# Sliding-window attention with a gated two-layer MLP on one core: w_in in three parts ahead of batch 1's Q and K, V's tail read once, the last PV inside stage one of tile 1

## The chip, the cores and the metric

One NeuronCore of a Trainium2 chip. The metric is the device time of one execution in microseconds (us). A profile's span is some 1.8 us shorter than the time of the same execution. Engines: PE is the matmul array (PEld its weight loads), DVE VectorE, ACT ScalarE, POOL GpSimd, SP SyncE.

## The reference

```python
# q, k, v: (8, 8, 576, 64) float32; w_in (512, 2048), w_out (2048, 512)
scores = q @ k.transpose(0, 1, 3, 2) / 8
rel = pos[:, None] - pos[None, :]
scores = where((rel >= 0) & (rel < 64), scores, -1e9)
a = softmax(scores) @ v
x = a.transpose(0, 2, 1, 3).reshape(4608, 512)
h = x @ w_in
out = (h * clip(h + 3, 0, 6) / 6) @ w_out
```

## The kernel before

The tokens are worked through in nine tiles of 512. For each, stage one (`s1`) makes 16 chunks of gated hidden features, four 512-column matmuls each, and stage two (`s2`) 16 chunks of output of the same size. The attention of later batches is fitted between these chunks, so that PE has work while DVE and ACT evacuate. A sequence of 576 is 4 blocks of 128 and a tail of 64 ("rest rows"; the attention work on those of batch 0 is called small). Scores are Q times K, PV is the softmax weights times V, a bank (h, o, acc or st) is one of PE's result buffers, and an evacuation is the copy out of one. A number in a line name such as L633 is a line of the kernel that ran, so the same code has other numbers in the other kernels.

The loads of weights and of batch 1 are all issued by POOL, into one queue, in this order:

```python
w_in = [load_w_in(0, 512, 0, NG)]
bt.cast_v(...); bt.cast_v(...)
w_in.append(load_w_in(512, 1024, 0, NG))
bt.cast_v(...)
w_in.append(load_w_in(1024, 1536, 0, NG))
ld = LoadsForPE(1, nc.gpsimd)
ld.main(0, 0, 4)                      # Q of batch 1, heads 0 to 3
ld.main(1, 0, 4)                      # K
w_in.append(load_w_in(1536, 2048, 0, NG))
ld.rest()                             # rest rows of Q and K
w_out = [load_w_out(0, 4)]
# ... later: Q and K of heads 4 to 7, w_out parts 2 and 3, rest rows of
# batch 0, w_out part 4, V of batch 1 (its last block with 128 rows)
```

The stretch that the change works on, in PE's order:

```python
run(m, 12)                            # the first chunks of stage one, tile 0
TT(bt, 0, oa_tr)                      # transposes of Q and K, head pair 0
run(m, 2)
TT(bt, 1)
run(m, 1)
RR(bt, st_tr(0))                      # transposes of the rest rows
run(m)
for h in range(0, H, 2):              # POOL: cast of V, all five blocks
    pcopy(out=bt.V[:, :, h : h + 2, 0:D], in_=vst1[:, :, h : h + 2, :])
# ...
m = s2(0, BY_PART)                    # go(n): n chunks of stage two, tile 0
go(); SS1_(0)                         # SS1_: scores, exp, mask of a pair
go(2); SS1_(1)
go(); TT(bt, 2, st_tr(0))
go(); TT(bt, 3, st_tr(1))
go(2); SS1_(2)
go(3)
SS1_(3)
go()
RR(bt0, st_tr(0))                     # batch 0's rest rows
acopy(...)                            # their V
go(2)
rest_s(bt0, 1)                        # small scores, exp, mask of batch 0's rest rows
go(2)
rest_n(bt0, 0)                        # their PV
pv_pair(bt, 0, 1)                     # PV of a head pair; X_: its transposes
go()
pv_pair(bt, 1, 0)
X_(bt, 0)
pv_pair(bt, 2, 1)
rest_x(bt0, h_tr())
X_(bt, 1, iter((tr_of(ps_o, "o"),)))
pv_pair(bt, 3, 0)
# then tile 1: m = s1(1, ...); run(m, 1); X_(.., 2); run(m, 1); X_(.., 3); ...
```

The softmax here doesn't subtract the row's maximum and nothing guards it: scores larger than these inputs give would overflow.

Of the kernel before, what the change touches and what calls it, by code (L numbers as in the profile page):

```python
# [24 lines left out]
def kernel(  # L25
# [10 lines left out]
    P = nc.NUM_PARTITIONS  # L36
    B, H, S, D = q.shape
    DM, FF = moe_w_in.shape
    NT = B * S
    NG = H // 2  # L40
    assert D == 64 and NG * P == DM and WINDOW == D
    KB = (S + P - 1) // P
    SP = KB * P
    R = 4
    SM = P * R
    SR = S - SM
# [17 lines left out]
    ps_o = ctx.enter_context(tc.tile_pool(name="ps_o", bufs=1, space=PSUM))  # L64
    ps_h = ctx.enter_context(tc.tile_pool(name="ps_h", bufs=1, space=PSUM))
    ps_acc = ctx.enter_context(tc.tile_pool(name="ps_acc", bufs=1, space=PSUM))
# [12 lines left out]
    def load_v(b, vst, h0, h1, eng=None):  # L79
        out = []  # L80
        for h in range(h0, h1):
            out.append((eng or nc.sync).dma_start(  # L82
                out=vst[:, 0 : KB - 1, h, :],
                in_=v[b, h, 0:SM, :].rearrange("(k p) d -> p k d", p=P),
            ))
        return out
# [35 lines left out]
    def load_v_by_head(b):  # L122
        vst = stage.tile([P, KB, H, D], F32, name="vst", tag="vst")
        ins = [nc.gpsimd.dma_start(
            out=vst[:, KB - 1, :, :], in_=v[b, :, S - P : S, :].rearrange("h s d -> s h d"),
        )]
        ins += load_v(b, vst, 0, H, nc.gpsimd)
        return vst, ins
# [43 lines left out]
    def keep_busy(n):  # L172
# [11 lines left out]
        out=mask1[:], in_=mask1[:], pattern=[[1, QW]], compare_op=ISGE,  # L184
# [3 lines left out]
        out=mask1[:], in_=mask1[:], pattern=[[-1, QW]], compare_op=ISGE,  # L188
# [7 lines left out]
    for o0, m0, m1 in ((0, 0, QW), (QW, 0, QW), (2 * QW, 0, QW), (3 * QW, 0, P), (3 * QW + P, WINDOW, P)):  # L196
        nc.vector.tensor_scalar(
            out=maskneg[:, o0 : o0 + m1 - m0], in0=mask1[:, m0:m1],
# [32 lines left out]
    def load_w_in(f0, f1, g0, g1):  # L231
        return nc.gpsimd.dma_start(
            out=win16[:, g0:g1, f0:f1],
            in_=moe_w_in[g0 * P : g1 * P, f0:f1].rearrange("(g p) f -> p g f", p=P),
        )

    def load_w_out(c0, c1):
        return nc.gpsimd.dma_start(
            out=wout16[:, c0:c1, :],
            in_=moe_w_out[c0 * P : c1 * P, :].rearrange("(c p) j -> p c j", p=P),  # L240
        )


    vcopy, pcopy, acopy = nc.vector.tensor_copy, nc.gpsimd.tensor_copy, nc.scalar.copy
# [95 lines left out]
    def tr_of(pool, name):  # L340
        return pool.tile([P, 1024], BF16, name=name)
# [81 lines left out]
    def pv_pair(bt, g, u):  # L423
        t = ps_st.tile([P, 2, 512], F32, name=f"st{u}")
        for h in range(2):
            pv(bt, g, h, t[:, h, :])
        ov = t[:, :, 0 : KB * VW].rearrange("p h (k w) -> p h k w", w=VW)
        rec = small.tile([P, 2, KB], F32, name="rec2")
        nc.vector.reciprocal(out=rec[:].unsqueeze(3), in_=ov[:, :, :, D:VW])
        opgs[bt.b, g] = opool.tile([P, KB, 2, D], BF16, name="opg")  # L430
        nc.vector.tensor_tensor(
            out=opgs[bt.b, g][:].rearrange("p k h d -> p h k d"), in0=ov[:, :, :, 0:D],
            in1=rec[:].unsqueeze(3).to_broadcast([P, 2, KB, D]), op=MULT,
        )
# [31 lines left out]
    def rest_n(bt, u):  # L466
        st = ps_st.tile([P, 2, 512], F32, name=f"st{u}")
        for h in range(2):
            o = st[:, h, :]
            for g in range(NG):  # L470
                nc.tensor.matmul(
                    o[0:SR, g * VW : (g + 1) * VW], lhsT=pTr[:, h, g * SR : (g + 1) * SR],
                    rhs=bt.V[:, KB - 1, 2 * g + h, :], start=True, stop=True,
                )
        ov = st[0:SR, :, 0 : NG * VW].rearrange("p h (g w) -> p h g w", w=VW)
        rec = small.tile([P, 2, KB], F32, name="rec2")
        rec = rec[0:SR, :, 0:NG]
        nc.vector.reciprocal(out=rec.unsqueeze(3), in_=ov[:, :, :, D:VW])
        nc.vector.tensor_tensor(
            out=opr[0:SR].rearrange("p g h d -> p h g d"), in0=ov[:, :, :, 0:D],  # L480
            in1=rec.unsqueeze(3).to_broadcast([SR, 2, NG, D]), op=MULT,
        )
# [27 lines left out]
    def h_bank():  # L510
        return ps_h.tile([P, 512], F32, name=h_name())

    def h_tr():
        return ps_h.tile([P, 1024], BF16, name=h_name())

    def s1_bank(fc, T):
        if T == 0:
            if fc in (6, 7, 14, 15):
                return (ps_o, ps_acc)[fc % 2].tile([P, 512], F32, name=("o", "acc")[fc % 2])[:]
            if fc in (8, 9, 12, 13):  # L520
                return ps_st.tile([P, 2, 512], F32, name=f"st{fc % 2}")[:, 0, :]
            return h_bank()[:]
        if T == 1:
            return turn()
        if T == 2:
            if fc in (8, 9):
                return ps_st.tile([P, 2, 512], F32, name=f"st{fc % 2}")[:, 0, :]
            if fc in (6, 7, 12, 13):
                return (ps_o, ps_acc)[fc % 2].tile([P, 512], F32, name=("o", "acc")[fc % 2])[:]
            return h_bank()[:]  # L530
        if T > 1 and fc < 2:
            return ps_st.tile([P, 2, 512], F32, name=f"st{fc}")[:, 0, :]
        if fc % 4 > 1:
            return h_bank()[:]
        return (ps_o, ps_acc)[fc % 4].tile([P, 512], F32, name=("o", "acc")[fc % 4])[:]
# [114 lines left out]
    def run(gen, n=10 ** 6):  # L650
        for _ in range(n):
            if next(gen, "end") == "end":
                break
# [29 lines left out]
    def X_(bt, g, banks=None):  # L683
        xt_pe(bt, g, next(banks) if banks else h_tr())()

    def TT(bt, g, banks=None):
        T_(bt, g, banks)
        do(bt, "q", g)
        do(bt, "k", g)

    def RR(bt, banks=None):
        R_(bt, banks)
        do(bt, "r")
# [13 lines left out]
    bt, st = Batch(0), stage0  # L707
# [3 lines left out]
    w_in = [load_w_in(0, 512, 0, NG)]  # L711
    bt.cast_v(vst0, 2, 4, pcopy)
    bt.cast_v(vst0, 4, 6, pcopy)
    w_in.append(load_w_in(512, 1024, 0, NG))
    bt.cast_v(vst0, 6, 8, pcopy)
    w_in.append(load_w_in(1024, 1536, 0, NG))
    ld = LoadsForPE(1, nc.gpsimd)
    ld.main(0, 0, 4)
    ld.main(1, 0, 4)
    w_in.append(load_w_in(1536, 2048, 0, NG))  # L720
    ld.rest()
    w_out = [load_w_out(0, 4)]
    pcopy(out=bt.V[0:SR, KB - 1, :, 0:D], in_=bt.V[SR:P, KB - 2, :, 0:D])

    def S0_(g, u):
# [2 lines left out]
    def T0_(g):  # L728
# [40 lines left out]
    m = s1(0, ((0, 1), (2,)))  # L769
# [11 lines left out]
        out=mask[:], in_=mask1[:].unsqueeze(1).to_broadcast([P, 2 * (KB - 1), QW])  # L781
    )
    for h in range(2):
        nc.vector.tensor_copy(
            out=mask[:, (KB - 1) * (h + 1) - 1, P:QW], in_=mask1[:, WINDOW : 2 * WINDOW],
        )
    bt, st = Batch(1), st1
    bt.cast_qk(st, 0, 0, 4, pcopy)
    bt.cast_qk(st, 1, 0, 4, pcopy)
    bt.cast_rest(st, pcopy)  # L790
    w_out += [load_w_out(4 * i, 4 * i + 4) for i in (1, 2)]
    rst0, rvst0 = load_rest_of_first()
    cast_pairs(bt, st, 4, 4)
    w_out.append(load_w_out(12, 16))
    vst1, insv = load_v_by_head(1)
    run(m, 12)

    def st_tr(u):
        t = ps_st.tile([P, 2, 1024], BF16, name=f"st{u}")
        return iter((t[:, 0, :], t[:, 1, :]))  # L800

    TT(bt, 0, oa_tr)
    run(m, 2)
    TT(bt, 1)
    run(m, 1)
    RR(bt, st_tr(0))
    run(m)

    for h in range(0, H, 2):
        pcopy(out=bt.V[:, :, h : h + 2, 0:D], in_=vst1[:, :, h : h + 2, :])  # L810
    st2, ins2 = load_for_dma(2, (0,))
    after(ins2[0], insv[3], "the values go first")
    ld = LoadsForPE(2, nc.sync)
# [9 lines left out]
    m = s2(0, BY_PART)  # L823
    def go(n=1):
        run(m, n)

    def SS1_(g):
        S1_(g, 0, 0)
        S1_(g, 1, 1)

    go()
    SS1_(0)
    go(2)
    SS1_(1)
    go()
    TT(bt, 2, st_tr(0))
# [1 line left out]
    TT(bt, 3, st_tr(1))  # L838
    go(2)
    SS1_(2)  # L840
    go(3)
    bt0.cast_rest((None, None, rst0), vcopy)
    SS1_(3)
    go()
# [1 line left out]
    acopy(out=bt0.V[SR:P, KB - 1, :, 0:D], in_=rvst0[SR:P, :, :])  # L846
    go(2)
    rest_s(bt0, 1)
    go(2)
    rest_n(bt0, 0)  # L850
    pv_pair(bt, 0, 1)
    go()
    pv_pair(bt, 1, 0)
    X_(bt, 0)
    pv_pair(bt, 2, 1)
    rest_x(bt0, h_tr())
    X_(bt, 1, iter((tr_of(ps_o, "o"),)))
    pv_pair(bt, 3, 0)

    def stage_(T, bt, pieces1, pieces2):  # L860
        if T < 3:
            m = s1(T, ((0,), (1,), (2,)))
            run(m, 1)
            X_(Batch(T), 2, oa_tr if T == 2 else st_tr(1))
            run(m, 1)
            X_(Batch(T), 3, oa_tr if T == 2 else st_tr(0))
            run(m, 1)
        else:
            m = s1(T)
        for i in range(NFC):  # L870
            run(m, 1)
            for f in pieces1.get(i, ()):
                f()
        m = s2(T, BY_BLOCK)
        for i in range(16):
            run(m, 1)
            for f in pieces2.get(i, ()):
                f()
# [42 lines left out]
    for T in range(1, NTB):  # L921
        p1, p2 = pieces(nxt)
        b = T + 2
        nxt = None
        if b < B:
# [13 lines left out]
            else:  # L939
                sts, _ = load_for_dma(b, (0, 1))  # L940
                vst = stage.tile([P, KB, H, D], F32, name="vst", tag="vst")
# [40 lines left out]
```

## Time and profile before

| | kernel before |
|---|---|
| time, median of the 3 runs given at first | 309.39 us (309.33 to 314.37) |
| span of the profile | 308.7 us |
| PE busy | 298.9 us, 97% |
| DVE, ACT, POOL busy | 57%, 57%, 32% |

In a timeline a row has its start, its length, engine, line, operation, what is written from what, and the number merged; a bracket gives the engine's idle time ahead of it and what ended it. Matmul ends are modelled about 0.17 us past the point where the next could start, so a stop counted start to start, as I do in the text, is that much longer than its bracket.

### The profile page before, as it was taken

Reading aid. Unit: us, or ns where it says so; the run is one execution under the profiler, and the core shown is the slowest. Engines: PE = TensorE matmul, PEld = TensorE weight load, DVE = VectorE, ACT = ScalarE, POOL = GpSimd, SP = SyncE. Lnnn points to the kernel's source line nnn. Section 1 sums busy time; section 2 is a strip of 40 time slices with the busy share of each in tenths; the row PEclk is TensorE's granted clock in tenths of the full one; section 3 lists DMA queues with packets and bytes.
Section 4 is the critical chain, followed back from the end, with each engine's and each line's share of the span. In section 5 each row is a group of like instructions: output and inputs, shape, how many; then the busy total and the mean of one; then the engine's idle time right before and its main releaser. Section 6 shows DMA issues by size and latency. Waiting matters only on the chain.

```text
span 308.7 us, 5635 instructions
## 1 busy us (share of the span) xinstructions
PE 298.9 (97%) x2158; PEld 150.5 (49%) x2194; DVE 174.7 (57%) x331; ACT 176.1 (57%) x266; POOL 98.5 (32%) x137
## 2 busy tenths in 40 slices
PE   8998999999999999999999999999999999999995
PEld 3454455644554454445444554455445544444444
DVE  4559644585736782677267834774477537306700
ACT  2858655686738851794179516961588157317711
POOL 4893785463534152407041704071400000000000
PEclk9999999999999999999999999999999999999999
DMA  7999999999999999999999979999910730010011
GB/s 239 192 191 258 254 203 206 244 186 288 199 220 235 220 201 200 230 218 210 196 256 210 217 162 250 220 205 156 242 51 0 132 92 0 34 70 34 0 70 68
DMA packets 140379, 52.94 MB, mean 171 GB/s; under 512 B 127584, under 2 KB 135136, under 8 KB 140352
## 3 DMA queue, kind: packets, MB, share of 16 engines
q1 hardware_dynamic: 134112, 42.94, 69.5%
q0 software_dynamic: 5824, 9.31, 14.5%
q8 instruction: 17, 0.28, 0.4%
q10 hardware_dynamic: 416, 0.33, 0.3%
q14 instruction: 10, 0.08, 0.1%
HBM read 36.83 MB, written 9.44 MB: 150 GB/s over the span
## 4 chain that ended last, share of the span: by engine, by line
PE 84%; DMA 9%; POOL 2%; SPq 1%; issue 1%; DVE 1%; ACT 0%; POOLq 0%
PE o L633 19%; PE h L567 17%; PE acc L633 17%; PE acc L567 6%; PE o L567 6%; PE st L567 6%; DMA rst<-in_k_dram 4%; PE st L364 4%; DMA wout<-in_moe_w_out_dram 3%; PE h L394 2%; DMA qst<-in_q_dram 2%; PE h L633 2%; PE h L399 1%; DMA vst<-in_v_dram 1%; SPq L82 1%
## 5 line engine op out<-in xcount | busy, mean ns | idle before, releaser
L567 PEld LDWEIGHTS <-win 128*128 128x128 bf16 x576 | 54.9, 98 | 64.5 <-DMA win<-in_moe_w_in_dram 1.2
L633 PEld LDWEIGHTS <-gT 128*128 128x128 bf16 x560 | 51.3, 98 | 57.4 <-DMA wout<-in_moe_w_out_dram 1.0
L633 PE MATMUL o<-wout,gT 128*128 128x512 bf16 x261 | 64.3, 380 | 0.7 <-issue 0.3
L567 PE MATMUL h<-xT,win 128*128 128x512 bf16 x254 | 62.4, 379 | 0.3
L633 PE MATMUL acc<-wout,gT 128*128 128x512 bf16 x245 | 58.3, 379 | 0.9 <-issue 0.5
L372 ACT ACTIVATE pT<-st 128x768 bf16<-128x768 f32 x64 | 48.5, 808 | 17.7 <-PE st L364 17.6
L575 DVE SCALAR_TENSOR_TENSOR gT<-t,st 128x512 bf16<-128x512 bf16 (+1 forms) x26 | 19.5, 767 | 56.6 <-ACT t L574 56.5
L575 DVE SCALAR_TENSOR_TENSOR gT<-t,h 128x512 bf16<-128x512 bf16 x65 | 43.8, 685 | 10.9 <-ACT t L574 10.7
L574 ACT ACTIVATE t<-h,half 128x512 bf16<-128x512 f32 x65 | 43.9, 691 | 7.7 <-PE h L567 7.5
L382 DVE TENSOR_TENSOR pT<-pT,mask 128x1536 bf16<-128x1536 bf16 x28 | 28.6, 1021 | 23.8 <-ACT pT L372 23.7
L639 ACT COPY osb<-acc 128x512 f32<-128x512 f32 x16 | 9.4, 586 | 42.7 <-PE acc L633 42.7
L253 POOL CAST V<-vst 128x2048 bf16<-128x2048 f32 (+1 forms) x10 | 13.9, 1387 | 52.5 <-DMA vst<-in_v_dram 43.4
L567 PE MATMUL st<-xT,win 128*128 128x512 bf16 x116 | 28.2, 379 | 0.9 <-DMA win<-in_moe_w_in_dram 0.8
L263 POOL CAST qn<-qst 128x512 bf16<-128x512 f32 x24 | 16.1, 709 | 40.2 <-DMA qst<-in_q_dram 38.4
L639 ACT COPY osb<-o 128x512 f32<-128x512 f32 x17 | 10.0, 589 | 29.4 <-PE o L633 28.3
L567 PE MATMUL acc<-xT,win 128*128 128x512 bf16 x98 | 25.7, 379 | 0.1
L567 PE MATMUL o<-xT,win 128*128 128x512 bf16 x95 | 25.1, 379 | 0.1
L416 DVE TENSOR_TENSOR opg<-h,rec 128x320 bf16<-128x320 f32 x48 | 23.6, 491 | 1.7
L574 ACT ACTIVATE t<-st,half 128x512 bf16<-128x512 f32 (+1 forms) x26 | 19.3, 754 | 6.0 <-PE st L567 5.6
L394 PEld LDWEIGHTS <-pT 128*128 128x128 bf16 x256 | 17.4, 97 | 7.5 <-PE h L440 0.5
L574 ACT ACTIVATE t<-acc,half 128x512 bf16<-128x512 f32 x25 | 17.2, 687 | 4.3 <-PE acc L567 3.6
L575 DVE SCALAR_TENSOR_TENSOR gT<-t,acc 128x512 bf16<-128x512 bf16 x25 | 17.1, 685 | 2.8 <-ACT t L574 2.8
(123 smaller groups left out, 301.8 us busy)
## 6 DMA issues: line engine op xcount, KB each, us to landing
out_dram<-osb SPq DMA_DIRECT2D x31, 256.0 KB, 2.5
qst<-in_q_dram SPq DMA_DIRECT2D x28, 256.0 KB, 4.8
vst<-in_v_dram SPq DMA_DIRECT2D x24, 256.0 KB, 5.3
kst<-in_k_dram SPq DMA_DIRECT2D x23, 256.0 KB, 5.5
win<-in_moe_w_in_dram POOLq DMA_DIRECT2D x4, 512.0 KB, 8.1
wout<-in_moe_w_out_dram POOLq DMA_DIRECT2D x4, 512.0 KB, 9.6
vst<-in_v_dram SPq DMA_DIRECT2D x14, 128.0 KB, 3.1
qst<-in_q_dram POOLq DMA_DIRECT2D x2, 512.0 KB, 11.9
```

The lines of the kernel that those rows point to most:

```text
L253: copy(out=self.V[:, 0 : KB - 1, h0:h1, 0:D], in_=vst[:, 0 : KB - 1, h0:h1, :])
L263: pcopy(out=n[:, g, 0 : KB - 1, :, :].rearrange("p k h d -> p k (h d)"), in_=s[:, 0 : KB - 1, 2 * g : 2 * g + 2, :].rearrange("p k h d -> ...
L364: nc.tensor.matmul(st[:, h, o0 : o0 + n], lhsT=bt.KT[h * D : (h + 1) * D, g, k0 : k0 + P], rhs=bt.QT[h * D : (h + 1) * D, g, q0 : q0 + n], ...
L372: nc.scalar.activation(out=pT[:, :, 2 * u : 2 * u + 2, 0:QW], in_=st[:, :, 0:w].rearrange("p h (k w) -> p h k w", k=2), func=EXP, scale=scale,
L382: nc.vector.tensor_tensor(out=pT[:, :, :, 0:QW], in0=pT[:, :, :, 0:QW], in1=mask[:].rearrange("p (h k) w -> p h k w", h=2), op=MULT,)
L394: nc.tensor.matmul(ob, lhsT=pT[:, h, qb, 0:P], rhs=V[:, qb, 2 * g + h, :], start=True, stop=(qb == 0),)
L416: nc.vector.tensor_tensor(out=opgs[bt.b, g][:, 0:nb, h, :], in0=ov[:, :, 0:D], in1=rec[:, 0:nb].unsqueeze(2).to_broadcast([P, nb, D]), op= ...
L567: nc.tensor.matmul(hT, lhsT=win16[:, g, fc * P : (fc + 1) * P], rhs=xT[:, g, t0 : t0 + TB], start=(g == 0), stop=(g == NG - 1),)
L574: nc.scalar.activation(out=t1[:], in_=hT, func=RELU, bias=half[:], scale=1.0 / 6.0)
L575: nc.vector.scalar_tensor_tensor(out=out, in0=t1[:], scalar=1.0, in1=hT, op0=MIN, op1=MULT,)
L633: nc.tensor.matmul(accs[ts], lhsT=gT[:, fc, ts * P : (ts + 1) * P], rhs=wout16[:, fc, :], start=(fc == 0), stop=(fc == NFC - 1),)
L639: acopy(out=osb[:], in_=accs[ts])
```

## The change

The intent: w_in comes ahead of Q and K, so that stage one need not wait for its fourth part; the first w_out part comes ahead of the rest rows; 64 rows of V that lie in two blocks are loaded once and copied on chip by ACT; the last PV fills time inside stage one. Cut to its core:

```diff
-            out=vst[:, KB - 1, :, :], in_=v[b, :, S - P : S, :]...
+            out=vst[SR:P, KB - 1, :, :], in_=v[b, :, SM:S, :]...
@@ banks of stage one's chunks in tile 0 changed to fit
-    w_in.append(load_w_in(512, 1024, 0, NG))
+    w_in.append(load_w_in(512, 1280, 0, NG))
     bt.cast_v(vst0, 6, 8, pcopy)
-    w_in.append(load_w_in(1024, 1536, 0, NG))
+    w_in.append(load_w_in(1280, 2048, 0, NG))
     ld.main(0, 0, 4)
     ld.main(1, 0, 4)
-    w_in.append(load_w_in(1536, 2048, 0, NG))
+    w_out = [load_w_out(0, 4)]
     ld.rest()
-    w_out = [load_w_out(0, 4)]
@@ w_out parts 2 and 3 are issued ahead of the cast of the rest rows
-    run(m, 12)
+    run(m, 14)
     TT(bt, 0, oa_tr)
-    run(m, 2)
-    TT(bt, 1)
-    run(m, 1)
-    RR(bt, st_tr(0))
     run(m)
+    RR(bt, iter((tr_of(ps_acc, "acc"),)))
+    bt.cast_v_end(vst1, pcopy)
     for h in range(0, H, 2):
-        pcopy(out=bt.V[:, :, h : h + 2, 0:D], in_=vst1[:, :, h : h + 2, :])
+        pcopy(out=bt.V[:, 0 : KB - 1, h : h + 2, 0:D], in_=vst1[:, 0 : KB - 1, h : h + 2, :])
+    def twice(g):
+        h = slice(2 * g, 2 * g + 2)
+        acopy(out=bt.V[0:SR, KB - 1, h, 0:D], in_=vst1[SR:P, KB - 2, h, :])
-    go()
+    go(2)
     SS1_(0)
     go(2)
+    TT(bt, 1, st_tr(0))
+    go()
     SS1_(1)
@@
     SS1_(2)
-    go(3)
+    go(2)
@@
     rest_s(bt0, 1)
-    go(2)
+    go()
     rest_n(bt0, 0)
+    twice(0)
     pv_pair(bt, 0, 1)
     go()
+    twice(1)
     pv_pair(bt, 1, 0)
     X_(bt, 0)
+    twice(2)
     pv_pair(bt, 2, 1)
     rest_x(bt0, h_tr())
-    X_(bt, 1, iter((tr_of(ps_o, "o"),)))
-    pv_pair(bt, 3, 0)
+    X_(bt, 1, iter((tr_of(ps_acc, "acc"),)))
+    twice(3)
@@ in stage one of tile 1, after its first four matmuls
+            if T == 1:
+                last_pv()          # pv_pair(bt, 3, 0)
```

More of the change, by code (lines that the diff above doesn't have):

```diff
@@ L124, in load_v_by_head @@
         ins = [nc.gpsimd.dma_start(
-            out=vst[:, KB - 1, :, :], in_=v[b, :, S - P : S, :].rearrange("h s d -> s h d"),
+            out=vst[SR:P, KB - 1, :, :], in_=v[b, :, SM:S, :].rearrange("h s d -> s h d"),
         )]
@@ L517, in s1_bank @@
         if T == 0:
-            if fc in (6, 7, 14, 15):
+            if fc in (6, 7, 10, 11):
                 return (ps_o, ps_acc)[fc % 2].tile([P, 512], F32, name=("o", "acc")[fc % 2])[:]
-            if fc in (8, 9, 12, 13):
+            if fc in (8, 9, 14, 15):
                 return ps_st.tile([P, 2, 512], F32, name=f"st{fc % 2}")[:, 0, :]
@@ L789 @@
     bt.cast_qk(st, 1, 0, 4, pcopy)
+    w_out += [load_w_out(4 * i, 4 * i + 4) for i in (1, 2)]
     bt.cast_rest(st, pcopy)
-    w_out += [load_w_out(4 * i, 4 * i + 4) for i in (1, 2)]
     rst0, rvst0 = load_rest_of_first()
@@ L848, with last_pv @@
     rest_s(bt0, 1)
-    go(2)
+    go()
     rest_n(bt0, 0)
+    twice(0)
     pv_pair(bt, 0, 1)
     go()
+    twice(1)
     pv_pair(bt, 1, 0)
     X_(bt, 0)
+    twice(2)
     pv_pair(bt, 2, 1)
     rest_x(bt0, h_tr())
-    X_(bt, 1, iter((tr_of(ps_o, "o"),)))
-    pv_pair(bt, 3, 0)
+    X_(bt, 1, iter((tr_of(ps_acc, "acc"),)))
+    twice(3)
+    def last_pv(bt=bt):
+        pv_pair(bt, 3, 0)
     def stage_(T, bt, pieces1, pieces2):
```

## The prediction

> **What bounds the kernel now.** I read the page's busy shares first, then the waits of TensorE, then the timelines of TensorE (PE), GpSimd (POOL) and ScalarE (ACT) over 18 to 60 us, where the change works, with the landing delay of each DMA issue there.
>
> ```profile
> PE 298.9 (97%) x2158; PEld 150.5 (49%) x2194; DVE 174.7 (57%) x331; ACT 176.1 (57%) x266; POOL 98.5 (32%) x137
> ```
>
> PE is busy nearly the whole span and the clock row of the page is full, so time is gained only where PE stands still. After 60 us the view of waits gives its matmuls 0.6 us of idle time in all, and none of that is put down to a DMA. Before that, three stops are put down to one:
>
> ```profile
> 21.95 1.89 PE L567 MATMUL h<-xT,win 128*128 128x512 bf16 x8
> 28.86 0.39 PE L327 MATMUL o<-ident,qn 128*128 128x128 bf16 x4
> ...
> 30.24 1.90 PE L567 MATMUL st<-xT,win 128*128 128x512 bf16 x8 [0.77 <-DMA win<-in_moe_w_in_dram]
> ...
> 33.28 0.39 PE L297 MATMUL st<-ident,rn 128*128 128x128 bf16 x4
> ...
> 35.00 1.04 PE L633 MATMUL h<-wout,gT 128*128 128x512 bf16 x4 [0.46 <-DMA wout<-in_moe_w_out_dram]
> ...
> 40.36 1.02 PE L633 MATMUL h<-wout,gT 128*128 128x512 bf16 x4 [0.16 <-DMA wout<-in_moe_w_out_dram]
> ```
>
> The bracket is idle time before the row. Counted start to start less the work (one 512-column matmul starts each 0.216 us), the stops are 0.93, 0.63 and 0.33 us: 1.9 us, the most that the reordering of loads can win. The rest rows of Q and K ("rn") are transposed at 33.28, shortly after their cast on POOL:
>
> ```profile
> 26.10 1.04 POOL L285 CAST qn<-qst 128x1024 bf16<-128x1024 f32 x1 [0.65 <-DMA qst<-in_q_dram]
> 27.54 1.04 POOL L285 CAST kn<-kst 128x1024 bf16<-128x1024 f32 x1 [0.40 <-DMA kst<-in_k_dram]
> 31.76 0.61 POOL L292 CAST rn<-rst 128x512 bf16<-128x512 f32 x1 [3.19 <-DMA rst<-in_k_dram]
> ```
>
> Issue time plus landing delay, one issue at a time, gives the order in which this one software queue delivered: w_in parts at 18.1 (12.02 + 6.1), 21.9 and 24.4, half of Q at 25.9, half of K at 27.4, w_in part four at 30.2 (17.92 + 12.3), rest of Q 31.1, rest of K 31.6 (19.80 + 11.8), first w_out part 35.0 (20.48 + 14.5), second halves of Q and K 36.4 and 37.9, second w_out 40.3, third 43.9. It is backlogged throughout, so order decides who waits, and a reordering makes nothing faster in sum. The end of this stretch is the other place:
>
> ```profile
> 50.09 0.58 ACT L639 COPY osb<-h 128x512 f32<-128x512 f32 x1 [0.93 <-PE h L633]
> 50.57 0.60 ACT L459 ACTIVATE pTr<-st 128x512 bf16<-128x512 f32 x1
> 51.28 0.58 ACT L639 COPY osb<-h 128x512 f32<-128x512 f32 x1
> 52.15 0.58 ACT L639 COPY osb<-o 128x512 f32<-128x512 f32 x1 [0.28 <-PE o L633]
> 53.97 0.58 ACT L639 COPY osb<-acc 128x512 f32<-128x512 f32 x1 [1.24 <-PE acc L633]
> 54.97 0.64 ACT L445 COPY xT<-h 128x576 bf16<-128x576 bf16 x1 [0.41 <-PE h L440]
> ```
>
> ```profile
> 49.98 0.29 PE L454 MATMUL st<-QT,KT 64*128 64x64 bf16 x8
> ...
> 52.04 0.44 PE L471 MATMUL st<-V,pTr 128*64 128x65 bf16 x8
> ...
> 52.91 1.03 PE L633 MATMUL acc<-wout,gT 128*128 128x512 bf16 x4
> 53.77 0.22 PE L394 MATMUL st<-V,pT 128*128 128x65 bf16 x2
> ...
> 54.48 0.45 PE L440 MATMUL h<-ident,opg 128*128 128x128 bf16 x5
> ```
>
> The reader is to see here that each evacuation on ACT starts 0.2 us after PE went on to other work (53.97 against 53.77) and takes 0.58, while PE never waits for it.
>
> **What the Trainium skill says.** "DMA: Bandwidth & Descriptors", section "Queues, rings and completion order": descriptors of one ring are consumed in ring order and the 16 engines finish independently. The landings agree for one queue (in order of issue, 0.5 to 3.7 us apart). Its section "Anatomy of one DMA" gives about 436 GB/s for the moving part; a w_in part reads 1.05 MB and two landings lie 2.6 to 3.7 us apart, 283 to 403 GB/s, so parts are near bandwidth and wider rows should buy little. "TensorE: Matmul & The Clock Gate", "Architectural detail", says that ACT is a strict FIFO; the ACT timeline keeps program order. "ScalarE: Activation LUTs", "What ACT_TABLE_LOAD costs", gives 186 ns + 0.833 ns per element without a pointer operand, back-to-back ones overlapping by some 93 ns: 612 ns for 512 elements, and the trace has 0.58 to 0.62.
>
> **Part 1, the order of loads.** The new order is w_in 512, 768, 768, Q, K, w_out 1, rest Q, rest K, then as before. The work of PE is the same.
> - The second w_in part is half as large again. It ends where half of the third part ended: 21.9 + (24.4 - 21.9)/2 = 23.15. PE wants it at 21.95, as before: +1.2 us of new stop.
> - The third part lands at 30.2 less the Q and K that no longer precede it (27.4 - 24.4 = 3.0): 27.2. It is wanted six chunks of 0.865 later, 23.15 + 5.2 = 28.35: no stop, so the 0.93 goes. Q and K move back by 2.8, to 28.7 and 30.2; K is cast by 31.4 and wanted after ten chunks, at 31.8: just in time.
> - The rest of K now ends where w_out 1 ended, near 35.0, plus the cast of 0.6: 35.6. PE reaches those transposes earlier. From 21.95 to 34.38 it had 12.43 us, less the stop of 0.93, the rest transposes 0.22 and one pair of transposes 0.45 that the change moves on: 10.83 of work. 23.15 + 10.83 = 34.0, so it stops about 1.6 us. w_out 1 (about 33.3) has landed by then and its stop goes, but stage two begins at 35.6 + 0.2 = 35.85 instead of 35.00, with the 0.45 of transposes still to do.
> - Then two chunks (1.73), scores 0.44, two chunks, the moved transposes 0.45: 40.2, just ahead of the second w_out at 40.3, so both kernels start that chunk near 40.4. Before had by then also done one scores (0.44) and one more transpose pair (0.45), 0.9 of work. The moved transposes sit one chunk (0.86) ahead of their scores while their copies on DVE and ACT take 0.7 + 0.6, so about 0.3 to 0.4 is lost there, and 0.3 of small stops of before is not met again. **Sum: about +1.0 us.**
>
> **Part 2, V's tail read once.** 128 KB less is loaded (about 0.5 us of the queue), but V is not what PE waits for: a pair was cast 1 us ahead of each PV in before. In exchange four ACT copies of 64x128 (186 + 107 = about 0.29 us, an estimate from the page above) each feed the last matmul of both halves of a PV, and they stand in ACT's order behind an evacuation.
> - PV of pair 1: chunk ends at 53.77 in the times of before, copy of acc 53.97 to 54.55, the new copy to about 54.75. PE wants it after seven small matmuls, 53.77 + 0.22: stop 0.75.
> - PV of pair 2: behind the xT copy 54.97 to 55.61, so 55.8; wanted at about 55.0: stop 0.8.
> - The small scores to small PV stretch loses one of two 0.86 chunks between them. Their chain (copy, exp 0.60, mask 0.42) made the result ready 1.65 us after 49.98; the new PE arrives after 0.23 + 0.86 = 1.1: stop 0.55. It also hides the first new copy.
> - The first chunk of stage one then waits for the copy of the batch 0 rest rows, late by the same queue: 0.25.
> **Sum: about +2.3 us.**
>
> **Part 3, the last PV inside stage one.** It covers the waits that PE had around 54.2 to 57.2, where 7.25 us held 6.85 of work: -0.3 to -0.4.
>
> Total +1.0 + 2.3 - 0.3 = +3.0 us. PE is full afterwards and no later wait is put down to a DMA, so I expect no absorption: 309.4 + 3.0 = 312.4. I shade it to 312.1, since the front half rests on landings that can shift.
>
> **Rivals.** (a) The intent holds: the stops of 1.9 us go, wide rows arrive faster than by bytes, and the ACT copies are slipped in during idle time: 307.5 to 308.5. For it: three stops are real, and ACT is idle 43%. Against: idle ACT does not help an in-order queue, and bandwidth near the limit leaves little for wider rows. (b) Only a part: w_in helps, the rest rows hurt, copies cost half: 309.5 to 311. (c) Worse than my sum: K's cast misses its slot at 31.8, or late reads of the V staging tile hold up batch 2's loads and its values are late in tile 1: 313.5 to 315. Against: its V cast sat idle 6.48 us for the load at 74.3 and PV came about 81, so some 5 us are spare.
>
> **Range and chances.** Rival (a) some 10%, (b) 25%, my sum 50%, (c) 15%. Faster by over 2% needs 303.2, more than all stops together: 1%. Slower by over 2% needs 315.6, twice my sum: 3%. Point 312.1, range 309.4 to 313.9.
>
> **What would show it.** In the changed profile: a w_in stop near 22 to 23 us and none before chunk 10; rn cast near 35 and an idle PE of over 1 us before its transposes; stage two starting after 35.4; the last matmul of the second and third PV starting only after a new ACT copy, 0.7 us or more late; the small PV of batch 0 waiting for pTr. If the rest of K lands before 34, or the new copies start before the evacuations, I am wrong by 1 to 2 us and (b) or (a) holds.

## More of the kernel before

The prediction shows the main rows. One more part of PE's timeline of before is needed later, the transposes of batch 1 around the start of tile 1:

```profile
55.59 0.45 PE L440 MATMUL o<-ident,opg 128*128 128x128 bf16 x5
...
56.37 0.60 PE L567 MATMUL h<-xT,win 128*128 128x512 bf16 x2
...
58.38 0.44 PE L440 MATMUL st<-ident,opg 128*128 128x128 bf16 x5
```

Between the first two rows stands the last PV, and the third follows the work ahead of it without idle time.

## The result and the profile after

The changed kernel takes 312.8 us (median of 6, 312.35 to 313.7), the kernel before 309.44 in the same set (308.96 to 314.37). The ratio of fast runs is 1.0105, 95% interval 1.0079 to 1.0132: slower, by about 3.3 us, inside 2%. The run of 314.37 us lies over 1.5% above the fastest of its kernel, so it counts as slow and is left out of the ratio. A ratio is the mean time of one kernel's fast runs over that of the other's of the same rounds, so not quite the ratio of the medians.

The span of the first profile after is 310.6 us. Its page, and PE's rows that answer to those of before:

```profile
PE 299.4 (96%) x2158; PEld 150.6 (48%) x2194; DVE 176.2 (57%) x331; ACT 177.0 (57%) x270; POOL 98.2 (32%) x137
```

```profile
21.87 1.89 PE L567 MATMUL h<-xT,win 128*128 128x512 bf16 x8
...
33.06 0.40 PE L297 MATMUL acc<-ident,rn 128*128 128x128 bf16 x4 [0.22 <-POOL rn L292]
...
38.12 1.02 PE L633 MATMUL h<-wout,gT 128*128 128x512 bf16 x4 [0.22 <-DMA wout<-in_moe_w_out_dram]
39.31 0.51 PE L364 MATMUL st<-QT,KT 64*128 64x192 bf16 x10 [0.16 <-ACT KT L332]
...
51.88 0.44 PE L471 MATMUL st<-V,pTr 128*64 128x65 bf16 x8 [0.79 <-DVE pTr L461]
...
54.65 0.19 PE L405 MATMUL st<-V,pT 128*128 128x65 bf16 x1 [0.66 <-ACT V L811]
...
56.28 0.19 PE L405 MATMUL st<-V,pT 128*128 128x65 bf16 x1 [0.71 <-ACT V L811]
```

The two L405 rows are the last matmuls of the first half of the second and third PV. Each waits for one of the new ACT copies, and ACT's timeline shows why they are late (CAST L811 is the new copy):

```profile
53.81 0.58 ACT L639 COPY osb<-acc 128x512 f32<-128x512 f32 x1 [1.91 <-PE acc L633]
54.30 0.30 ACT L811 CAST V<-vst 64x128 bf16<-64x128 f32 x1
55.40 0.64 ACT L445 COPY xT<-h 128x576 bf16<-128x576 bf16 x1 [0.80 <-PE h L440]
55.93 0.30 ACT L811 CAST V<-vst 64x128 bf16<-64x128 f32 x1
```

ACT stood idle for 1.91 us ahead of the evacuation, with V's rows in place (the last of them landed at 50.9), but the copy came behind the evacuation in its order. So a small copy of 0.30 us cost PE 0.82 us, and the next one 0.88.

The front is another matter. In this pair of profiles it looks better than before: no stop at w_in, and 0.39 us at the rest rows where I expected 1.6. But the first profile of before was of a run of 310.5 us, 1.1 over its median, and its load queue had begun 0.95 us later (first issue at 12.02, against 11.07). One profile of each was not enough, so both kernels were profiled once more.

### The profile page after: what moved, and what is told of

The parts are those of the page before. It is cut to its first block, busy times and chain, and to the rows that moved or that the text cites. A ratio compares the mean times of both kernels' runs of the same rounds, so it can differ in the third digit from the quotient of the medians.

```text
span 310.6 us, 5645 instructions
## 1 busy us (share of the span) xinstructions
PE 299.4 (96%) x2158; PEld 150.6 (48%) x2194; DVE 176.2 (57%) x331; ACT 177.0 (57%) x270; POOL 98.2 (32%) x137
## 4 chain that ended last, share of the span: by engine, by line
PE 85%; DMA 7%; POOL 2%; ACT 2%; issue 1%; SPq 1%; DVE 1%; POOLq 0%
PE o L633 19%; PE acc L633 17%; PE h L567 17%; PE acc L567 6%; PE st L567 6%; PE o L567 6%; DMA rst<-in_k_dram 4%; PE st L364 4%; PE h L633 2%; PE h L394 2%; DMA qst<-in_q_dram 1%; PE h L399 1%; DMA vst<-in_v_dram 1%; SPq L82 1%; PE h L615 1%
```

## The experiments

Three numbers are read in each profile. *First landing* is the time from the issue of the first w_in part to its landing. *Front* is from that issue to the start of the small scores of batch 0 (`rest_s`); where 14 chunks of stage two stand ahead of them instead of 13, one chunk of 0.865 us is taken off. *Back* is from there to the first weight load of tile 1's stage two, with that chunk added. So kernels with different orders can be compared; front plus back holds the same work in all of them. The runs of before are shared by the four kernels from before_again to pv_only, by no_v to early_two, and by once_early to wout_first.

| kernel | first landing | front | back | time against before, ratio (95%) |
|---|---|---|---|---|
| before | 6.1 | 37.97 | 21.23 | |
| before_again | 7.0 | 37.91 | 21.29 | 0.9996 (0.9945 to 1.0047) |
| after | 5.5 | 37.89 | 23.98 | 1.0105 (1.0079 to 1.0132) |
| after_again | 6.4 | 38.72 | 23.63 | 1.0116 (1.0075 to 1.0157) |
| loads_only | 6.1 | 38.69 | 21.76 | 1.0052 (1.0009 to 1.0096) |
| v_only | 5.8 | 38.04 | 23.88 | 1.0071 (1.0024 to 1.0118) |
| pv_only | 7.8 | 39.27 | 21.68 | 1.0011 (0.9956 to 1.0066) |
| no_v | 6.5 | 38.58 | 22.20 | 1.0071 (1.0031 to 1.0111) |
| two_chunks | 7.7 | 39.79 | 23.45 | 1.0110 (1.0069 to 1.0152) |
| early_copies | 6.2 | 38.83 | 22.53 | 1.0097 (1.0050 to 1.0145) |
| early_two | 8.2 | 40.03 | 21.69 | 1.0090 (1.0037 to 1.0143) |
| once_early | 7.6 | 37.72 | 22.38 | 1.0004 (0.9972 to 1.0035) |
| rest_first | 7.8 | 40.46 | 21.68 | 1.0050 (1.0020 to 1.0081) |
| wout_first | 6.5 | 37.23 | 21.25 | 1.0055 (1.0008 to 1.0103) |

All results were correct. Two properties of the table carry the reading: the back moves little between two profiles of one kernel (0.06 and 0.35 us; where the 0.35 comes from stands at early_copies), and the front of the new order depends on the first landing, which differs by chance. The intervals reach about 1 to 1.7 us to each side, more than most pairs of theories differ by. So where a measured time is said below to be as a theory had it, this is said of its mean; what decides is the profile. Nor do all runs have the same mean granted clock (0.987 to 1.000). With the runs at 0.998 or more alone, on both sides, no difference of a changed kernel changes its sign: +3.0 us for v_only, +2.7 for no_v and early_copies, +3.9 for two_chunks and after_again, +0.2 for once_early. The unchanged before_again stands at +0.6 there, which shows what such differences are worth.

**before_again**: the kernel before with a comment added.

> The kernel before, unchanged, for a second profile. The first one was of a run of 310.5 us, 1.1 us over the median. Theory A (the load queue of that one execution was late by about 1 us, so part of the front gain of the changed kernel is chance): its first w_in part lands near 17 us instead of 18.2, the fourth w_in part and the first w_out are waited for less than 0.93 and 0.63 us, and the span is near 307.7. Theory B (the new order itself delivers faster): landings as in the first profile within 0.3 us and the same three stops. Ratio 1.000 +- 0.002 either way.

The queue began at 11.20, but the first part took 7.0 us and landed at 18.2 as in the first profile. Its stops at DMA:

```profile
29.66 1.90 PE L567 MATMUL st<-xT,win 128*128 128x512 bf16 x8 [0.23 <-DMA win<-in_moe_w_in_dram]
39.49 1.02 PE L633 MATMUL h<-wout,gT 128*128 128x512 bf16 x4 [0.52 <-DMA wout<-in_moe_w_out_dram]
```

Start to start these are 0.40 and 0.69 us. The stop at the first w_out is gone and the one at the second has grown; in sum they are 0.8 us less than in the first profile. The front is 37.91 against 37.97 all the same, since it is counted from the issue, and the first part landed 0.8 us later after that. Neither theory was right about the landings. The span of 308.0 is nearer to A's 307.7 than to the 308.7 of the first profile.

**loads_only**: the changed kernel with part 2 and part 3 undone.

```diff
-            out=vst[SR:P, KB - 1, :, :], in_=v[b, :, SM:S, :]...
+            out=vst[:, KB - 1, :, :], in_=v[b, :, S - P : S, :]...
-    bt.cast_v_end(vst1, pcopy) ; casts of 4 blocks ; twice(0) .. twice(3)
+    casts of 5 blocks
-    last_pv() in stage one of tile 1; X_(bt, 1) in acc
+    pv_pair(bt, 3, 0) ahead of it; X_(bt, 1) in o
```

> Part 1 alone: the new order of loads and the new places of transposes, scores and chunks, without the ACT copies of V's tail and with the last PV where it was. Theory A (the back half costs the time, the front is about even): +0.0 to +1.0 us against before, of which 0.8 is the small PV of batch 0 that waits for its mask since one chunk fewer lies ahead of it. Theory B, as the prediction had it (the front costs 1.0, that chunk 0.55 and the xT copy 0.25): +1.5 to +2.0 us. If the front gains all its stops: -0.5 or less.

Measured +1.6 us (0.52%), as theory B had it, the prediction's own; the interval of 0.3 to 3.0 reaches into A's range as well. In its profile PE stops 0.75 us at the wide w_in part, 1.33 at the rest rows, 0.71 at the scores behind the moved transposes and 0.61 at the small PV. Front +0.8, back +0.5.

**v_only**: the kernel before with V's tail loaded once and the four ACT copies, one directly ahead of each PV.

> Part 2 alone on the kernel before: V's tail read once, four ACT copies. Theory A (each copy stands behind an evacuation in ACT's order and PE waits for it): here none is hidden: about 0.45 for PV 0, 0.8 each for PV 1 and 2, 0.6 for PV 3: +2.2 to +2.8 us, and in the profile the last matmul of each PV waits for ACT. Rival (128 KB less in the queue is worth more than the copies cost, or the waits overlap others): -0.5 to +0.7.

Measured +2.2 us (0.71%), theory A. The view of waits has all four:

```profile
PE st L405 <- ACT V L814: 2.3, 4, 0.7
```

Start to start they are 0.34, 0.82, 0.88 and 0.88, in sum 2.92, and the back is 2.6 longer. By the backs this is the dearest of the three parts taken alone. In the changed kernel the first and the last of the four copies are covered, so part 2 costs less there (see no_v).

**pv_only**: the kernel before with the last PV inside stage one of tile 1.

> Part 3 alone on the kernel before: the last PV inside stage one of tile 1. As predicted: -0.2 to -0.4 us, since the stretch held 0.4 us of small stops. Rival (the last PV now sits close before the transposes that need it, so a new wait on the DVE multiplication takes the place): 0 to +0.4.

In time +0.1% with an interval of +-0.55%, so the times don't tell. The profile does, for the back: +0.4 us, the rival's figure.

```profile
56.50 0.59 PE L567 MATMUL h<-xT,win 128*128 128x512 bf16 x2
...
59.21 0.45 PE L440 MATMUL st<-ident,opg 128*128 128x128 bf16 x5
```

Both rows have no bracket, yet the first starts 0.22 us later than the work ahead of it needs (it waits for ACT's copy of the rest rows) and the second 0.20 (it waits for DVE's multiplication of that PV). In before the PV stood ahead of the first and covered the copy, and its own multiplication had longer. loads_only and no_v differ by part 3 alone, and their backs by 0.44: the same.

**no_v**: the changed kernel with part 2 undone (the first two pairs of lines of loads_only's diff).

> The changed kernel with part 2 undone: V's tail loaded twice and cast by POOL as before. Theory A (the ACT copies cost two stops of 0.82 and 0.88 us on PE): 1.5 to 1.8 us less than the changed kernel, +1.4 to +1.9 against before; no wait of PV for ACT in the profile. Rival (PE would wait at the same places for DVE or V's casts): within 0.5 of the changed kernel, +2.8 to +3.3.

Measured +2.2 us (0.71%); A had +1.4 to +1.9, the rival +2.8 to +3.3, and the interval of 1.0 to 3.4 us covers both. The profile decides: no PV waits for ACT, and the back is 1.4 to 1.8 shorter than in the two profiles of the changed kernel.

**two_chunks**: the changed kernel, one chunk moved back to between small scores and small PV.

```diff
     SS1_(2)
-    go(2)
+    go()
@@
     rest_s(bt0, 1)
-    go()
+    go(2)
     rest_n(bt0, 0)
```

> The changed kernel with one chunk moved from ahead of the last scores to between the small scores and the small PV of batch 0, as in before. Theory A (the 0.95 us stop at the small PV is the chain copy, exp, mask that one chunk cannot cover): the stop goes, but the first ACT copy that it hid shows up with about 0.4: -0.4 to -0.9 against the changed kernel, +2.4 to +2.9 against before. Rival (the stop only moves to the small scores, which wait for the mask of the last scores): no change, +3.0 to +3.4.

+3.4 us (1.10%), as the rival had it, though the interval of 2.1 to 4.7 covers A too. The stop at the small PV fell to 0.18, but the first PV now waits 0.26 for its copy, which the stop had hidden, and ahead of the small scores the scores of the last pair stop 0.36 for an exp and the rest rows' transposes 0.19. In sum these come to 1.0 us, as much as the 0.95 of the first profile of the changed kernel: the move mostly changed who waits.

**early_copies**: the changed kernel with the copies ahead of the evacuations.

```diff
     acopy(out=bt0.V[SR:P, KB - 1, :, 0:D], in_=rvst0[SR:P, :, :])
+    twice(0)
+    twice(1)
     go(2)
     rest_s(bt0, 1)
     go()
+    twice(2)
+    twice(3)
     rest_n(bt0, 0)
-    twice(0) .. twice(3) ahead of each PV
```

> The changed kernel with the four ACT copies moved ahead: two behind the copy of batch 0's V rows, two ahead of the small PV, instead of behind the evacuations. Same work. Theory A (order on ACT, not its load, costs the time): the two PV stops go, -1.5 to -1.8 against the changed kernel, +1.4 to +1.9 against before, about the same as with part 2 undone. Rival (ACT's load counts, or the copies now wait for V's loads and hold up the evacuations): -0.5 to +0.5 against the changed kernel.

```profile
50.03 0.50 ACT L811 CAST V<-vst 64x128 bf16<-64x128 f32 x2
...
52.61 0.49 ACT L811 CAST V<-vst 64x128 bf16<-64x128 f32 x2
```

The same four copies now run in pairs, no PV waits for ACT, and the back is 1.1 to 1.5 us shorter than in the changed kernel. That is theory A, on the trace. The time, +3.0 us with an interval of 1.5 to 4.5, has its mean where the rival had it and does not show the gain. In this profile the wide w_in part was waited for by 1.14 us.

The stop at the small PV, 0.94 us here, is a case of its own. The mask of the small scores (DVE, L461) takes 0.42 or 0.43 us in the seven profiles in which no cast of POOL was running when it began, after_again and no_v among them. In the other seven it began during one and ended 0.26 or 0.27 us after the end of such a cast, so it took 0.57 to 0.86 us: 0.77 in the first profile of the changed kernel, 0.76 here. No run tests whether the cast is the cause. But like can be compared with like: with the long mask the back fell from 23.98 to 22.53 (early_copies), with the short one from 23.63 to 22.20 (no_v), by 1.4 us each time. So in the changed kernel the place of the copies costs as much as the whole of part 2.

**early_two**: the edits of early_copies and two_chunks together.

> Both mends: copies early and two chunks between small scores and small PV. Theory A: the stops are gone together, about -2.6 to -3.0 against the changed kernel, so -0.5 to +0.6 against before: what is left is the front half. If the front were worth the -1.0 that the pair of profiles shows: -1.0 to -0.5.

The back is 21.69, 1.9 to 2.3 less than in the changed kernel and only part 3's 0.4 above before. The time, +2.8 us (interval 1.1 to 4.4), is far above what A expected, and A fails here: it took the front for even. The front of this profile is 40.03, 2.1 above before. Some 0.5 of that is not the queue's: as in two_chunks, the moved chunk puts two stops ahead of the small scores that are not in the changed kernel (0.36 and 0.19).

**once_early**: the kernel before with part 2, the copies placed as in early_copies.

> The kernel before with V's tail read once (part 2), but the ACT copies ahead of the evacuations. Theory A (the copies cost only through their place in ACT's order): the four stops of 0.34, 0.82, 0.88 and 0.88 us of v_only are gone, +0.0 +- 0.3 us against before and 2.2 to 2.8 less than v_only; the 128 KB less win nothing since V is not waited for. Rival (reading the tail once costs in itself, by V coming later or by the load on ACT): +1.0 to +2.0.

310.45 against 310.38 us, ratio 1.0004, interval -0.9 to +1.1 us: no difference seen, where v_only lost 2.2. The profile corrects the reason, though. The back is 1.1 longer, since here the copies came too early:

```profile
49.13 0.30 ACT L814 CAST V<-vst 64x128 bf16<-64x128 f32 x1 [0.87 <-DMA vst<-in_v_dram]
50.21 0.30 ACT L814 CAST V<-vst 64x128 bf16<-64x128 f32 x1 [0.77 <-DMA vst<-in_v_dram]
```

```profile
52.28 0.44 PE L471 MATMUL st<-V,pTr 128*64 128x65 bf16 x8 [1.07 <-DVE pTr L461]
```

ACT waited for V's loads with the copies at the head of its order, and the exp of the small scores behind them came late. That this is not in the mean time means that not every execution meets it, or that it lies within the interval of +-1 us; it is not settled.

**rest_first**: loads_only with `ld.rest()` ahead of the first `load_w_out` again.

> loads_only with the rest rows of Q and K loaded ahead of the first w_out part, as in before. Theory A (the wide w_in part and then the late rest rows are the stops of the new front; both trade against the first w_out, all in one queue): the stop at the rest rows, 0.84 to 1.33 us in the profiles of loads_only and no_v, falls under 0.3, the first w_out is waited for by 0.2 to 0.6 instead, and the later stops at the second w_out stay: -0.2 to -0.8 us against loads_only. Rival (the rest rows cost nothing, the second w_out binds anyway): within 0.2 of loads_only, and in the profile the time goes over to the stop at the second w_out in full.

+1.5 us (0.50%), the same mean as loads_only, as the rival had it; the interval of 0.6 to 2.5 covers A's gain too. By the profile the time does go elsewhere, and not to the second w_out alone:

```profile
32.59 0.40 PE L327 MATMUL acc<-ident,kn 128*128 128x128 bf16 x4 [0.72 <-POOL kn L285]
...
35.66 1.90 PE L633 MATMUL h<-wout,gT 128*128 128x512 bf16 x8 [0.61 <-DMA wout<-in_moe_w_out_dram]
...
40.95 1.02 PE L633 MATMUL h<-wout,gT 128*128 128x512 bf16 x4 [0.68 <-DMA wout<-in_moe_w_out_dram]
```

The stop at the rest rows is 0.11; K's cast, the first and the second w_out are waited for instead. With w_in ahead of all, everything behind it in the one queue is late, whichever comes first.

**wout_first**: an attempt at a faster version, the kernel before with the second w_out part issued ahead of Q and K of heads 4 to 7, and their transposes three chunks later.

```diff
+    w_out.append(load_w_out(4, 8))
     ld.main(0, 4, 8)
     ld.main(1, 4, 8)
@@
-    w_out += [load_w_out(4 * i, 4 * i + 4) for i in (1, 2)]
+    w_out.append(load_w_out(8, 12))
@@
-    go()                # ahead of TT(bt, 2, ..)
+    go(4)
@@
-    go(2)               # ahead of SS1_(2), then go(3)
+    go()                #                    then go()
```

> The kernel before with the second w_out part issued ahead of the second halves of Q and K, and their transposes three chunks later. If the front of before is bound by the landing of the second w_out (0.33 us of stop in the first profile, 0.69 in the second, 1.08 in v_only's): that stop goes, -0.3 to -1.0 us against before. Rival (the third w_out or the later Q and K take its place): -0.1 to +0.5.

The stop at the second w_out is gone and the front is the shortest of all, 37.23, but the time is +1.7 us (0.55%, interval 0.2 to 3.2): above both expectations, so the attempt failed. Its profiled run, 310.28 us, was the fastest of its six. One new wait is seen far from the edit:

```profile
122.89 1.24 PE L567 MATMUL st<-xT,win 128*128 128x512 bf16 x5 [0.62 <-DMA xT<-opg]
```

Whether this wait, 0.79 us start to start, comes of the shift is open.

**after_again**: the changed kernel with a comment added.

> The changed kernel, unchanged, for a second profile and more times. In the profiles so far the first w_in part landed 5.5 (changed kernel, first profile) to 8.2 us after its issue, by chance, and the small scores of batch 0 began 0.7 to 0.8 us later for each us of that in kernels with the new order, while those with the old order hardly moved up to about 7.6. Theory A (the front costs 0.1 us at a first landing of 5.5 and 1 to 2 us at 7.5; the back costs 2.7 always): small scores to the first chunk of tile 1's stage two 23.0 to 23.2 us as in the first profile; small scores at issue plus 38.8 + 0.75 x (first landing - 5.5) within 0.5; times +3.2 to +4.5 against before. Rival (the front is about even, as the first profile had it): the small scores within 0.3 of issue plus 38.8 whatever the first landing is, times +2.5 to +3.2.

```profile
22.36 1.90 PE L567 MATMUL h<-xT,win 128*128 128x512 bf16 x8 [0.49 <-DMA win<-in_moe_w_in_dram]
...
33.98 0.40 PE L297 MATMUL acc<-ident,rn 128*128 128x128 bf16 x4 [0.64 <-POOL rn L292]
...
40.23 0.51 PE L364 MATMUL st<-QT,KT 64*128 64x192 bf16 x10 [0.54 <-ACT KT L332]
...
52.45 0.44 PE L471 MATMUL st<-V,pTr 128*64 128x65 bf16 x8 [0.44 <-DVE pTr L461]
```

+3.6 us (1.16%), in A's range and above the rival's, though the interval of 2.3 to 4.9 covers both. The small scores began 39.59 us after the issue; A's formula gives 39.4, the rival 38.8. The stretch behind them, 22.76, is 0.24 under A's range, since the small PV waited 0.61 and not 0.95. With this profile and before_again the bill closes: PE's stops of over 0.1 us from the first w_in matmul on to tile 1 are 4.93 us here (0.66, 0.81, 0.71, 0.61, 0.82, 0.88, 0.24, 0.20) and 1.71 there (0.40, 0.12, 0.69, 0.15, 0.22, 0.13), a difference of 3.2. From that matmul to tile 1's stage two the profiles differ by 3.1 (55.27 and 52.18), and the other 0.4 of the spans' 3.5 (311.5 and 308.0) lies behind.

A further stop of 0.22 us seems to stand in the two profiles of the changed kernel, here as in the first:

```profile
57.39 0.59 PE L567 MATMUL h<-xT,win 128*128 128x512 bf16 x2
58.05 0.38 PE L567 MATMUL acc<-xT,win 128*128 128x512 bf16 x1
```

It is none. Each turn of this stage has four matmuls, and the one into o has no record here, while its weight load has one (57.83). In two_chunks, where it is recorded, the fourth starts 0.44 us behind the second, just as here.

## Why the prediction was right, and where it was wrong

The measured 312.8 lies in the range and 0.4 us from the unshaded sum of 312.4. Step by step, with the two profiles of the changed kernel as first / second:

- **The wide w_in part, +1.2.** 0 / 0.66, and 0.75 to 1.14 in loads_only, no_v and early_copies; 0.15 or less in two_chunks, early_two and rest_first, where the first part landed after 7.7 us or more and PE had waited 0.7 to 1.4 for it already. The mechanism is there; the size hangs on the first landing, 5.5 / 6.4 us. The predicted loss of the stop for the old fourth part holds in all.
- **The rest rows, 1.6.** 0.39 / 0.81, and 1.33 in loads_only. The queue ran faster than I had read it from the one profile of before: from the first issue to the landing of the last of the same loads, 22.9 us there, 21.2 / 22.0 here. That profile was one draw from a spread of 2.7 us in the first landing alone, and I took it for the rule.
- **K's cast just in time.** No stop in both, as predicted, but with 1.1 / 1.0 us to spare and not 0.4: again the queue was faster.
- **Scores behind the moved transposes, 0.3 to 0.4.** 0.33 / 0.71, of which 0.1 stands ahead of every scores row in before too.
- **Front in sum, +1.0.** -0.1 / +0.8 by the profiles. Old orders kept 37.7 to 38.0 for first landings from 5.8 to 7.6 us (of the 39.3 of pv_only 1.7 has another cause, in the last section); new ones went from 37.9 at 5.5 over 38.6 to 38.8 at 6.1 to 6.5 to about 39.3 and 39.5 at 7.7 and 8.2 (the 39.8 and 40.0 of two_chunks and early_two, less the 0.5 of their moved stops; rest_first, a third order, had 40.5 at 7.8). As I read these few points, the old front takes a late queue up, the new one hands it on to PE. This I had not seen, and it makes the front cost more in a usual run than in the first profile.
- **ACT copies, 0.75 and 0.8.** 0.82 and 0.88 in both profiles. Right, as was the first copy being hidden behind the small PV's stop. The estimate of 0.29 us for a copy was 0.30 in the trace.
- **The small PV, 0.55.** 0.95 / 0.61. Right in kind: the difference between the two profiles is the mask on DVE, 0.77 / 0.42, where I had taken the 0.42 of before.
- **The xT copy, 0.25.** 0.24 in both.
- **The last PV inside stage one, -0.3 to -0.4.** This step was wrong, in sign: "It covers the waits that PE had around 54.2 to 57.2, where 7.25 us held 6.85 of work". The waits in before that I counted, 0.22 and 0.12 us, stand ahead of X_1 and stay. A third of 0.22 is one matmul that the trace has no record of, not a wait. In their place the PV uncovered one copy and sits too close before its own transposes: +0.4 us (pv_only, and no_v less loads_only).
- **No absorption after 60 us.** Right: from tile 1's stage two to the end before took 237.5 and 237.6 us, after 237.7 and 238.0.

The prediction also named a sign of being wrong by 1 to 2 us: the rest of K landing before 34. It landed at 32.3 / 33.2, and stage two began at 33.3 / 34.2, not after 35.4, and yet the total held. The errors of the front (too dear by 0.2 to 1.1 us) and of the last PV (too cheap by 0.7) partly cancelled, so the good total is in part luck. Back in sum: predicted +2.3 - 0.3 = +2.0, measured +2.7 / +2.3.

What stays open: the times resolve about +-1.3 us, so the gains of the mends are shown in traces and not in times; no mended version is shown to beat the kernel before. Its best equal is once_early.

## What to carry to other kernels

Before giving a small operation to an engine that is half idle, look at what stands ahead of it in that engine's order and when that is released: 0.3 us of copying cost PE 0.8 because an evacuation was in front, and too early a place blocks the engine on a load. Where one backlogged queue feeds everything, moving one load forward only chooses who waits; ask also which order still works when the queue starts a microsecond late. And take two profiles of a kernel before reading effects under 1 us from one.

## What the Trainium skill lacked or had wrong

- "TensorE: Matmul & The Clock Gate", section "Why this matters for your kernels", advises "No PE-idle gaps >~3µs between matmul bursts". In pv_only a gap of 1.3 us was followed by a drop: the first w_in part came late, and the granted clock, the third number from the right in these rows, went to a half for some 3.5 us:

```profile
18.00:19.00 1.00, 0.01 (x1) 0.02 (x2) 0.97 (x4) 0.29 (x1) 1.00 (x2) 0.77 1.18 193
20.00:21.00 1.00, 1.00 (x4) 0.30 (x2) 0.00 (x0) 0.00 (x0) 0.61 (x1) 0.50 1.25 208
22.00:23.00 1.00, 1.00 (x9) 0.57 (x8) 0.00 (x0) 0.40 (x1) 0.48 (x1) 1.00 1.12 351
```

  Gaps of 1.03 to 1.24 us at the same place (early_two, once_early, rest_first) had no such drop. That the gap alone did it is not shown: in the three us ahead of it PE was busy for 0.5 to 0.8 of each. In pv_only's set, runs of before at a mean clock of 0.994 or 0.995 took 311.2 to 312.8 us, those at 0.998 or more 308.6 to 310.3. In once_early's set it does not go so: 310.5 and 310.6 at 0.994, and up to 311.6 at 1.000.
- "DMA: Bandwidth & Descriptors", section "Anatomy of one DMA", gives one fit, 2.0 us plus bytes at 436 GB/s, an estimate of 4.4 us for the 1.05 MB that a w_in part reads. The first part took 5.5 to 8.2 us from issue to landing over 14 profiles. V's loads were in flight at the same time, so the longer times do not contradict the fit; but the page gives no figure for the spread of one transfer over executions, and its cause is open here.
- No page says that a matmul without a record in the trace looks like a stop of one matmul (0.22 us), with the idle bracket near 0.05. In the prediction I took one for a wait, and the rows at 57.39 and 58.05 above are another.
